# A linear-attention and two-MoE kernel on one core: the second part's preparation drawn one operation at a time, and new orders of the first loads and steps

## The chip, the cores and the metric

The kernel runs on one core of a Trainium2 chip. The time is the device time of one execution in microseconds, taken as the median of several runs. The engines named below are PE (TensorE), DVE (VectorE), ACT (ScalarE), POOL (GpSimd) and SP (SyncE, which issues all the DMAs here).

## What is computed

```python
kv  = einsum('bhsd,bhse->bhde', k, v);  o = einsum('bhsd,bhde->bhse', q, kv)     # 8 batches, 8 heads, 576 tokens, 64
x   = (o / sqrt(mean(o*o, -1) + 1e-6) * g_norm)  -> [4608, 512]
h   = x @ w_in                                             # [4608, 2048]
g   = (a0 + a1 h + a2 h^2 + a3 h^3) / (1 + |b0||h| + |b1|h^2 + 1e-6)
x2  = g @ w_out                                            # [4608, 512]
out = ((x2 @ w1) * (x2 @ w2) @ w3) @ w_out2                # [4608, 512]
```

The weights arrive in float64 and are turned into float32 on the chip. A float32 product is made of three passes, with each operand split into a rounded high part (`hi`) and a rest (`lo`): `hi*hi + hi*lo + lo*hi`.

## The kernel before

The program is written in a fixed order, and each engine works through its own list in that order. What an engine's next instruction needs from another engine is a semaphore wait, and everything behind it on the same engine waits too.

**The opening (lines 449 to 461)** is a string of letters, one operation each: `W` loads one weight block of 512 KB (float64, lines 99 to 115), `C` converts the next loaded block, `K` loads one tile of 128 tokens of k and v (512 KB), `Q` one of q (256 KB), `k` makes the tile's part of `kv` on PE, `t` transposes q, `o` multiplies it by `kv`, `r` and `n` normalise, `x` writes the split tile of x, `c` and `d` are constants, `F` finishes the pending conversions. A conversion is four steps (`to_f32`, lines 144 to 161): one on ACT (L149) and three on DVE (L151, L155, L159). The split of a converted block (L84 on ACT, L85 on DVE) follows when two more blocks have been converted. The k, v and q tiles have two buffers each, so the third `K` waits on SP until the first `k` has read its tile, and all loads behind it in SP's list wait with it. Eleven blocks are converted in the opening and 21 in the first 23 steps.

**The first MoE (lines 1103 to 1135)** goes through NG = 192 steps: 12 blocks of 384 tokens with 16 slices of the hidden width each. In step g PE makes `h` of slice g (`l1`, 12 matmuls) and adds slice g-3 to the four output accumulators (`l2`, 12 matmuls). `h` has two PSUM banks. Between them lies the rational function, written as generators that `mix` interleaves by a string of letters: `n` is `ew1` of slice g (three on ACT, L535 to L537; one on POOL, L539; then L542 and L544 on DVE, which read `h` from PSUM), `y` is `ewy` of slice g (two on ACT, after POOL), `s` is `ew2` of slice g-1 (L558, L560, L562 on DVE), `l` is `ew3` of slice g-2 (hi on ACT L525, lo on DVE L527), and `t`, `u`, `v` are conversions. `MIX` (line 1042) has one string for the first 23 steps and one for the rest; `CONV` (line 1043) says how many blocks are converted in each of the first 23 steps.

**The second part (lines 652 to 836)** multiplies x2 by w1 and w2 in `c_slot(n)`, 48 slots of seven products of six matmuls (five in the first slot). It is a fast 2x2 matrix scheme: seven combinations of the weights (A11, A12, A22, S1 to S4) and seven of the x2 blocks (B11, T1 to T4, B21, B22), each made by subtractions on DVE and a split (cast on ACT, rest on DVE). Slots 0 and 1 use the weights of `cw(0)`, 2 and 3 those of `cw(1)`. They take over the first MoE's buffers as these come free: the weights' combinations the `wa`/`wb` slots, the x2 pieces the x tiles and the buffers of the rational function.

**How this preparation is ordered before (lines 1065 to 1076).** LB = 176 is the first step of the last block. `prep` runs whole groups of operations at the head of a step, ahead of the step's own: loads at LB+1 and LB+7, the 11 operations of `cw(0)` in steps 185 to 190, the x2 pieces B11 in 187, the subtractions T3, T1, T2 in 188, the split T3 in 190, T1, T4's subtraction and T2 at 192. What is left is run inside `c_slot(0)` and `c_slot(1)` from `extra1` and `extra2`, between the products, all of `cw(1)` among it (in `c_slot(0)`). `c_slot(0)` stands in step 192, ahead of the last two `l2`; after the last one `x2_out` copies the four accumulators and stores them.

Of the kernel before, what the change touches and what calls it, by code (L numbers as in the profile page):

```python
# [8 lines left out]
F32 = mybir.dt.float32  # L9
# [3 lines left out]
AF = mybir.ActivationFunctionType  # L13
ALU = mybir.AluOpType
# [4 lines left out]
def linear_attention_two_moe_kernel(  # L19
# [24 lines left out]
    nc = tc.nc  # L44
# [4 lines left out]
    P = 128  # L49
# [4 lines left out]
    TA = 384  # L54
# [10 lines left out]
    wp = ctx.enter_context(tc.tile_pool(name="wp", bufs=1))  # L65
# [14 lines left out]
    def f32(ap):  # L80
        return ap.bitcast(F32)
# [325 lines left out]
    with tc.manual_schedule():  # L407
# [23 lines left out]
        def w_next():  # L431
            kind, i = w_seq[n_cv[0]]
            n_cv[0] += 1
            return (conv_a if kind == "a" else conv_b)(i)
# [16 lines left out]
            "r": (n_rms, n_rsq), "n": (n_out, x_pe), "x": (x_out,),  # L451
        }
        whole = {"W": w_load, "C": w_conv, "F": conv_flush, "c": consts, "d": const_ops}
        for op in "QKWQWKCWKWcCkCKKCQdtkWkktFktWCWooQoWWrCCWtWCoKWKrWnrkrKnCnQKkCxnxxWQCxWW":
            if op in whole:
                whole[op]()
            else:
                i = count.get(op, 0)
                count[op] = i + 1
                for f in tile_ops[op]:  # L460
                    f(i)
# [56 lines left out]
        def mt(tag, bufs, dt=F32):  # L518
            return mp.tile([P, TA], dt, tag=tag, name=tag, bufs=bufs)
# [55 lines left out]
        def do(g, place):  # L575
            for f, i in todo.get((g, place), ()):
                f(i)
# [69 lines left out]
        def sub(out, x, y):  # L647
            nc.vector.tensor_tensor(out=out, in0=x, in1=y, op=ALU.subtract)
# [4 lines left out]
        A11, A12, A22, S1, S2, S3, S4 = range(7)  # L653
        B11, T3, T1, T2, B21, T4, B22 = range(7)
        IP = 2
        cw = {}
        w12q = w12d.rearrange("(i s) p f -> s p i f", s=2)

        def cw_load(ip):
            def quad(t, row, half):  # L660
                nc.sync.dma_start(
                    out=t.rearrange("p (i f) -> p i f", i=IP),
                    in_=w12q[row][:, ip * IP:(ip + 1) * IP, half * 2 * P:(half + 1) * 2 * P],
                )
            e = cw[ip] = {m: slot(ip * 7 + m) for m in range(3)}
            for m, row, half in ((A11, 0, 0), (A12, 0, 1), (A22, 1, 1)):
                quad(f32(e[m][1]), row, half)
            t = wp.tile([P, 2, W], F32, tag=("wb0", "wb8", "wb9", "wb14")[ip], name="cwt")
            e["r"], e["t"] = t[:, 0, :], t[:, 1, :]
            quad(e["r"], 1, 0)  # L670

        def cw_work(ip):

            e = cw[ip]

            def to(m, t):
# [36 lines left out]

        raws = {}
# [3 lines left out]
        def raw_x(j, names=("11", "12", "22", "21")):  # L718
            if j >= NPR:
                return  # L720
            r = raws.setdefault(j, {})
            for name, tag, half, blk in RAW:
                if name not in names:
                    continue
                if tag:
                    r[name] = [atp.tile([P, TA], F32, tag=tag, name="xr", bufs=2) for _ in range(2)]
                else:
                    t = wp.tile([P, 2, TA], F32, tag="wb13" if j else "wb10", name="xr21")
                    r[name] = [t[:, kk, :] for kk in range(2)]
                for kk in range(2):  # L730
                    c0 = (2 * j + blk) * TA
                    nc.sync.dma_start(out=r[name][kk], in_=x2d[2 * half + kk, :, c0:c0 + TA])

        def gen_tmp(j):
            r = raws[j]
            t = wp.tile([P, 2, TA], F32, tag="wb14" if j else "wb7", name="xt3")
            r["tmp"] = [t[:, kk, :] for kk in range(2)]

        def gen_work(j):
# [299 lines left out]
                nc.scalar.copy(f["u"], f["b"])  # L1039
            e_load(n + 3)  # L1040

        MIX = "usnttulnslyutsntutu", "nltysstnnltts"
        CONV = "21102011020121111110011"
        NG = NBA * MF
        LB = NG - MF
        prep = {}
        extra1, extra2 = {}, {}

        def add(d, n, *fs):
            d.setdefault(n, []).extend(fs)  # L1050
# [3 lines left out]
        def take(key, *ns):  # L1054
            def f():
                if key not in work:
                    kind, n = key
                    work[key] = cw_work(n) if kind == "cw" else gen_work(n)
                for n in ns:
                    fs = work[key][n]  # L1060
                    for x in fs if isinstance(fs, list) else [fs]:
                        x()
            return f

        add(prep, LB + 1, lambda: raw_x(0, ("11", "12", "22")))
        add(prep, LB + 7, lambda: cw_load(0))
        for n in range(11):
            add(prep, LB + 9 + n // 2, take(("cw", 0), n))
        add(prep, LB + 11, take(("x", 0), 0))
        add(prep, LB + 12, take(("x", 0), 1, 2, 3))  # L1070
        add(prep, LB + 14, lambda: raw_x(0, ("21",)), take(("x", 0), 4))
        add(prep, NG - 1, lambda: cw_load(1))
        add(prep, NG, take(("x", 0), 5, 6, 7))
        add(extra1, 0, take(("x", 0), 8), take(("cw", 1), 0, 1, 2, 3, 4))
        add(extra2, 0, take(("cw", 1), 5, 6, 7, 8, 9, 10))
        add(extra1, 1, take(("x", 0), 9, 10), lambda: cw_load(2))
        add(extra2, 2, lambda: cw_load(3))
        for n, ip in ((2, 2), (4, 3)):
            add(extra1, n, take(("cw", ip), 0, 1, 2, 3))
# [2 lines left out]
        for j in range(NPR):  # L1082
# [8 lines left out]
            if j:  # L1091
                for c in range(5):
                    n = 5 * (j - 1) + c
# [7 lines left out]
        add(extra1, last + 7, lambda: w3_load(0))  # L1101

        for g in range(NG + SK):
            for f in prep.get(g, ()):
                f()
            do(g, 0)
            gens = {}
            if g < NG:
                l1(g)
                do(g, 1)  # L1110
                gens["n"] = ew1(g)
            if 0 <= g - 2 < NG:
                gens["l"] = ew3(g - 2)
            if g < NG:
                gens["y"] = ewy(g)
            if 0 <= g - 1 < NG:
                gens["s"] = ew2(g - 1)
# [8 lines left out]
            mix("".join(x for x in MIX[g >= len(CONV)] if x in gens), **gens)  # L1126
# [63 lines left out]
```

## Time and profile before

| | us |
|---|---|
| median of 3 runs | 1608.46 (1608.38 to 1609.85) |
| the profiled execution's own time | 1611.97 |
| its span, first to last instruction | 1609.6 |
| PE busy | 1532.3 (95%) |
| DVE busy | 1301.8 (81%) |
| ACT busy | 1057.8 (66%) |
| POOL busy | 230.1 (14%) |

Busy time is the time in which an engine had an instruction running. The granted clock is the share of full speed (2.4 GHz) that PE was given; its other level is one half (1.2 GHz). In the rows below a time at the head of a row is in microseconds from the start of the span, and the brackets at the end give the idle time of the engine ahead of that instruction and what released it.

### The profile page before, as it was taken

Reading aid. Unit: us, or ns where it says so; the run is one execution under the profiler, and the core shown is the slowest. Engines: PE = TensorE matmul, PEld = TensorE weight load, DVE = VectorE, ACT = ScalarE, POOL = GpSimd, SP = SyncE. Lnnn points to the kernel's source line nnn. Section 1 sums busy time; section 2 is a strip of 40 time slices with the busy share of each in tenths; the row PEclk is TensorE's granted clock in tenths of the full one; section 3 lists DMA queues with packets and bytes.
Section 4 is the critical chain, followed back from the end, with each engine's and each line's share of the span. In section 5 each row is a group of like instructions: output and inputs, shape, how many; then the busy total and the mean of one; then the engine's idle time right before and its main releaser. Section 6 shows DMA issues by size and latency. Waiting matters only on the chain.

```text
span 1609.6 us, 26146 instructions
## 1 busy us (share of the span) xinstructions
PE 1532.3 (95%) x9640; PEld 1482.0 (92%) x9640; DVE 1301.8 (81%) x2373; ACT 1057.8 (66%) x2109; POOL 230.1 (14%) x201
## 2 busy tenths in 40 slices
PE   3699999999999999999999997999999999999999
PEld 3588899999999999999999996999999998789999
DVE  3999977879899999999898989776676675578885
ACT  3588777778888888787888886444344343455554
POOL 0022121212222222222222221000000000000000
PEclk9699999999999999999999999999999999999999
DMA  9736234331111111111101011434533533344442
GB/s 258 206 99 168 63 95 112 86 92 45 42 44 52 47 37 47 46 53 27 53 27 55 6 47 36 151 109 150 184 125 125 183 116 130 118 131 158 158 158 86
DMA packets 202079, 157.93 MB, mean 98 GB/s; under 512 B 122848, under 2 KB 179936, under 8 KB 201952
## 3 DMA queue, kind: packets, MB, share of 16 engines
q1 hardware_dynamic: 201952, 156.28, 32.6%
q8 instruction: 75, 1.23, 0.3%
q14 instruction: 52, 0.43, 0.1%
HBM read 106.43 MB, written 49.81 MB: 97 GB/s over the span
## 4 chain that ended last, share of the span: by engine, by line
PE 71%; DVE 18%; ACT 5%; issue 3%; SPq 1%; POOL 1%; DMA 1%; DVEq 0%; ACTq 0%; POOLq 0%
PE acc L779 11%; PE h L88 6%; PE h L90 6%; PE h L89 6%; PE acc L492 5%; PE acc L987 5%; PE acc L489 5%; PE acc L490 5%; PE h L779 5%; PE kv L779 3%; PE at L779 3%; DVE n L560 3%; PE h L987 2%; DVE n L562 2%; DVE n L542 2%
## 5 line engine op out<-in xcount | busy, mean ns | idle before, releaser
L539 POOL TENSOR_TENSOR s<-z,a 128x384 f32<-128x384 f32 x192 | 228.5, 1190 | 759.5 <-ACT z L536 411.9
L560 DVE SCALAR_TENSOR_TENSOR n<-n,na,y 128x384 f32<-128x384 f32 x192 | 180.9, 942 | 0.0
L551 ACT ACTIVATE y<-s,epsq 128x384 f32<-128x384 f32 x192 | 118.4, 617 | 71.5 <-POOL s L539 70.9
L542 DVE TENSOR_TENSOR n<-n,h 128x384 f32<-128x384 f32 x192 | 104.8, 546 | 57.5 <-ACT n L537 57.0
L536 ACT ACTIVATE z<-a,ab 128x384 f32<-128x384 f32 x192 | 136.1, 709 | 6.4
L537 ACT ACTIVATE n<-h,na 128x384 f32<-128x384 f32 x192 | 126.0, 656 | 5.1 <-DVE lo L527 5.0
L535 ACT ACTIVATE a<-h 128x384 f32<-128x384 f32 x192 | 93.4, 487 | 54.3 <-PE h L90 52.9
L558 DVE SCALAR_TENSOR_TENSOR s<-s,y 128x384 f32<-128x384 f32 x192 | 125.1, 651 | 1.0
L544 DVE SCALAR_TENSOR_TENSOR n<-n,na,h 128x384 f32<-128x384 f32 x192 | 117.8, 613 | 6.0
L562 DVE SCALAR_TENSOR_TENSOR n<-s,n 128x384 f32<-128x384 f32 x192 | 105.8, 551 | 0.0
L527 DVE TENSOR_TENSOR lo<-n,hi 128x384 fp32r<-128x384 f32 x192 | 105.7, 551 | 0.0
L552 ACT ACTIVATE y<-y 128x384 f32<-128x384 f32 x192 | 101.0, 526 | 6.1
L525 ACT CAST hi<-n 128x384 fp32r<-128x384 f32 x192 | 96.3, 502 | 8.5 <-DVE n L562 8.3
L269 PEld LDWEIGHTS kv<-vt,kt 128*64 128x64 f32 (+1 forms) x640 | 25.1, 154 | 30.1 <-issue 21.3
L269 PE MATMUL kv<-vt,kt 128*64 128x64 f32 (+1 forms) x640 | 30.9, 246 | 20.0 <-DMA vt<-in_v_dram 18.1
L821 ACT COPY p<-kv 128x384 f32<-128x384 f32 x24 | 11.5, 479 | 41.3 <-PE kv L779 29.9
L821 ACT COPY p<-acc 128x384 f32<-128x384 f32 x24 | 11.5, 480 | 38.4 <-PE acc L779 33.0
L350 PE MATMUL at<-kvbd,qT 128*128 128x128 f32 (+1 forms) x216 | 28.9, 284 | 7.0 <-ACT qT L342 4.2
L350 PEld LDWEIGHTS at<-kvbd,qT 128*128 128x128 f32 (+1 forms) x216 | 26.6, 183 | 8.9 <-ACT qT L342 5.2
L836 ACT COPY u<-acc 128x384 f32<-128x384 f32 x24 | 11.5, 480 | 33.6 <-PE acc L779 33.6
L375 ACT ACTIVATE ny<-ms,epsn 128x8 f32<-128x8 f32 x36 | 11.1, 308 | 33.8 <-DVE ms L369 33.7
L796 DVE TENSOR_TENSOR acc<-acc,u 128x384 f32<-128x384 f32 x24 | 13.6, 566 | 19.2 <-ACT u L836 18.8
(1408 smaller groups left out, 4960.0 us busy)
## 6 DMA issues: line engine op xcount, KB each, us to landing
ed<-eo SPq DMA_DIRECT2D x48, 384.0 KB, 2.6
er<-ed SPq DMA_DIRECT2D x36, 512.0 KB, 3.8
x2d<-xev SPq DMA_DIRECT2D x48, 192.0 KB, 2.0
xr<-x2d SPq DMA_DIRECT2D x48, 192.0 KB, 4.2
out_dram<-o SPq DMA_DIRECT2D x36, 256.0 KB, 2.2
qt<-in_q_dram SPq DMA_DIRECT2D x32, 256.0 KB, 3.1
kt<-in_k_dram SPq DMA_DIRECT2D x32, 256.0 KB, 3.4
vt<-in_v_dram SPq DMA_DIRECT2D x32, 256.0 KB, 4.1
```

Source lines behind the costliest of these rows:

```text
L527: nc.vector.tensor_tensor(out=e["lo"], in0=e["n"], in1=f32(e["hi"]), op=ALU.subtract)
L536: nc.scalar.activation(out=z, in_=a, func=AF.Identity, scale=ab[:, 1:2], bias=ab[:, 0:1])
L537: nc.scalar.activation(out=n, in_=h, func=AF.Identity, scale=na[:, 3:4], bias=na[:, 2:3])
L539: nc.gpsimd.tensor_tensor(out=s, in0=z, in1=a, op=ALU.mult)
L542: nc.vector.tensor_tensor(out=n, in0=n, in1=h, op=ALU.mult)
L544: nc.vector.scalar_tensor_tensor(out=n, in0=n, scalar=na[:, 1:2], in1=h, op0=ALU.add, op1=ALU.mult)
L551: nc.scalar.activation(out=y, in_=e["s"], func=AF.Abs_reciprocal_sqrt, bias=epsq[:, 0:1])
L558: nc.vector.scalar_tensor_tensor(out=s, in0=s, scalar=EPS_Q, in1=y, op0=ALU.add, op1=ALU.mult)
L560: nc.vector.scalar_tensor_tensor(out=n, in0=n, scalar=na[:, 0:1], in1=y, op0=ALU.add, op1=ALU.mult)
L562: nc.vector.scalar_tensor_tensor(out=n, in0=s, scalar=2.0, in1=n, op0=ALU.subtract, op1=ALU.mult)
L779: nc.tensor.matmul(bank, lhsT=lh[:, sl], rhs=x, start=first and kk == 0 and n == 0, stop=kk == 1 and n == 2, skip_group_check=True,)
L987: nc.tensor.matmul(bank, lhsT=l[:, c, :], rhs=r, start=first and c == 0 and x == 0, stop=c == KH - 1 and x == 2, skip_group_check=True,)
```

## The change

There are three edits.

1. The opening has a new order of the same letters. The first weight block is now loaded ahead of the first k and v tile; three `K` stand ahead of the second weight block; the constants are loaded before the first conversion; the conversions of the second to the sixth block, the transposes and the normalisation are ordered anew. Ten of the eleven conversions stood ahead of the last `x` that the first `h` needs; now nine do.
2. The first 23 steps have a new string in `MIX` (in `n`, `u`, `n` first, where it was `u`, `s`, `n`) and a new `CONV` (again 21 conversions in all).
3. The preparation is one chain of 76 single operations in a fixed order (`UNITS`). Each unit has the first step in which it may start (its gate). From step 177 on, `t` in the step's string draws the next operation of the chain; `PREP` says how many are drawn at most in each step, and drawing stops at a closed gate. The last block has a third `MIX` string, in which L542 and L544 stand ahead of L527 and L560. What is left is run in `c_slot(0)`, `(1)` and `(2)`, up to a given unit. Two scratch tiles move to other slots (`wb1`, `wb2` for `wb7`, `wb10`).

```diff
-        for op in "QKWQWKCWKWcCkCKKCQdtkWkktFktWCWooQoWWrCCWtWCoKWKrWnrkrKnCnQKkCxnxxWQCxWW":
+        for op in "QWKKKWcCCdtQkQWKkKWWCFkCtkWkWCCCWoCtQWWrKtCooWronrrnknWxxKnxWKWCkKQQCxWW":
...
-        MIX = "usnttulnslyutsntutu", "nltysstnnltts"
-        CONV = "21102011020121111110011"
+        MIX = "nunutsstlyltstntuuu", "nltysstnnltts", "ntsnnltlsyttst"
+        CONV = "21011011120111120111110"
...
-        add(prep, LB + 1, lambda: raw_x(0, ("11", "12", "22")))
-        add(prep, LB + 7, lambda: cw_load(0))
-        for n in range(11):
-            add(prep, LB + 9 + n // 2, take(("cw", 0), n))
-        add(prep, LB + 11, take(("x", 0), 0))
-        add(prep, LB + 12, take(("x", 0), 1, 2, 3))
-        add(prep, LB + 14, lambda: raw_x(0, ("21",)), take(("x", 0), 4))
-        add(prep, NG - 1, lambda: cw_load(1))
-        add(prep, NG, take(("x", 0), 5, 6, 7))
-        add(extra1, 0, take(("x", 0), 8), take(("cw", 1), 0, 1, 2, 3, 4))
-        add(extra2, 0, take(("cw", 1), 5, 6, 7, 8, 9, 10))
-        add(extra1, 1, take(("x", 0), 9, 10), lambda: cw_load(2))
+        def c_first(ip):
+            yield from u_c(ip, "f1")
+            yield from u_c(ip, "f2")
+            yield from u_to(ip, S3, "r")
+            yield from u_to(ip, S1, "t")
+            yield from u_c(ip, "f3")
+            yield from u_in(ip, A11)
...
+        UNITS = [
+            (LB + 1, lambda: half(raw_x, 0, ("11", "12", "22"))),
+            (LB + 2, lambda: u_piece(B11, "11")),
+            (LB + 4, lambda: half(cw_load, 0)),
+            (LB + 4, lambda: u_sub("tmp", "22", "12")),
+            (LB + 5, lambda: u_sub("12", "12", "11")),
+            (LB + 5, lambda: u_sub("11", "22", "12")),
+            (LB + 7, lambda: c_first(0)),
+            (LB + 7, lambda: c_rest(0)),
+            (LB + 4, lambda: u_piece(T3, "tmp")),
+            (LB + 14, lambda: half(cw_load, 1)),
+            (LB + 5, lambda: half(raw_x, 0, ("21",))),
+            (LB + 7, lambda: u_sub("tmp", "11", "21")),
+            (NG, lambda: u_piece(T1, "12")),
+            (NG, lambda: u_piece(T2, "11")),
+            (NG + 1, lambda: u_piece(B21, "21")),
+            (NG, lambda: c_first(1)),
+            (NG + 2, lambda: u_piece(T4, "tmp")),
+            (NG + 2, lambda: u_piece(B22, "22")),
+            (NG, lambda: c_rest(1)),
+        ]
+        PREP = "0623342432431864785"
...
+        add(extra1, 0, u_upto(13))
+        add(extra2, 0, u_upto(15))
+        add(extra1, 1, u_upto(18), lambda: cw_load(2))
+        add(extra1, 2, u_upto(19))
...
+            if LB < g:
+                gens["t"] = u_some(int(PREP[g - LB]))
+            mix("".join(x for x in MIX[(g >= len(CONV)) + (g > LB)] if x in gens), **gens)
```

## Rows read from the trace of the kernel before

**Rows 1.** Busy time of each engine by stretch (us), then clock, DMA share, GB/s.
```profile
0.00:62.30 62.30, 29.13 (x227) 24.88 (x228) 34.93 (x68) 25.70 (x49) 2.17 (x10) 0.81 0.93 237
62.30:190.00 127.70, 114.97 (x766) 104.62 (x765) 125.70 (x226) 103.15 (x195) 31.95 (x23) 0.96 0.50 130
960.50:1009.50 49.00, 37.73 (x187) 35.10 (x186) 45.63 (x79) 31.87 (x63) 7.14 (x6) 0.93 0.09 30
```

**Rows 2.** Waits of DVE, 0 to 63 us: total, times, longest.
```profile
DVE wa0r L151 <- DMA wa0r<-in_moe_w_in_dram: 8.9, 1, 8.9
DVE wa2hl L85 <- ACT wa2hl L84: 4.1, 1, 4.1
DVE wa4r L155 <- ACT ct L149: 3.8, 1, 3.8
DVE wb0r L155 <- ACT ct L149: 3.0, 1, 3.0
DVE n L542 <- ACT n L537: 2.0, 1, 2.0
```

**Rows 3.** Timeline of PE and DVE, the first tile and weight blocks as they land.
```profile
6.31 1.12 PE L269 MATMUL kv<-vt,kt 128*64 128x64 f32 x16 [6.31 <-DMA vt<-in_v_dram]
...
8.87 0.43 DVE L151 TENSOR_SCALAR wa0r<-wa0r 128x512 int32<-128x512 uint32 x1 [8.87 <-DMA wa0r<-in_moe_w_in_dram]
...
18.92 0.43 DVE L151 TENSOR_SCALAR wa3r<-wa3r 128x512 int32<-128x512 uint32 x1 [1.26 <-DMA wa3r<-in_moe_w_in_dram]
```

**Rows 4.** Timeline of DVE: a conversion, a split, pairs of 384 columns.
```profile
41.05 0.42 DVE L151 TENSOR_SCALAR wa5r<-wa5r 128x512 int32<-128x512 uint32 x1
...
42.92 0.68 DVE L85 TENSOR_TENSOR wa4hl<-ct,wa4hl 128x512 fp32r<-128x512 f32 x1
...
992.61 1.02 DVE L85 TENSOR_TENSOR xq<-xr,xq 128x384 fp32r<-128x384 f32 x2
993.55 1.02 DVE L648 TENSOR_TENSOR xt<-xr,xr 128x384 f32<-128x384 f32 x2
```

**Rows 5.** Timeline of PE: starts of steps 181, 182 and 187, then of c_slots.
```profile
935.28 0.34 PE L88 MATMUL h<-xh,wa5hl 128*128 128x384 f32 x1
939.48 0.34 PE L88 MATMUL h<-xh,wa6hl 128*128 128x384 f32 x1
960.48 0.34 PE L88 MATMUL h<-xh,wa11hl 128*128 128x384 f32 x1
...
1009.50 0.34 PE L779 MATMUL acc<-xq,wa0hl 128*128 128x384 f32 x1
1018.96 0.34 PE L779 MATMUL at<-xq,wa7hl 128*128 128x384 f32 x1
1026.33 0.34 PE L779 MATMUL acc<-xq,wa7hl 128*128 128x384 f32 x1
```

**Rows 6.** Timeline of DVE and POOL: a free step, a loaded one, an early one.
```profile
938.91 1.02 POOL L539 TENSOR_TENSOR s<-z,a 128x384 f32<-128x384 f32 x1 [3.18 <-ACT z L536]
939.42 0.55 DVE L542 TENSOR_TENSOR n<-n,h 128x384 f32<-128x384 f32 x1 [1.06 <-ACT n L537]
...
955.88 1.38 DVE L560 SCALAR_TENSOR_TENSOR n<-n,na,y 128x384 f32<-128x384 f32 x1
...
129.32 3.26 POOL L539 TENSOR_TENSOR s<-z,a 128x384 f32<-128x384 f32 x1 [3.77 <-ACT z L536]
```

**Rows 7.** Timeline of PE and DVE, the last l2 and the first two c_slots.
```profile
1005.74 0.48 PE L489 MATMUL acc<-hi,wb15hl 128*128 128x384 f32 x1 [4.54 <-ACT hi L525]
...
1011.32 0.56 DVE L798 TENSOR_TENSOR c<-h,p 128x384 f32<-128x384 f32 x1 [4.56 <-DMA x2d<-xev]
...
1018.61 0.57 DVE L796 TENSOR_TENSOR acc<-acc,u 128x384 f32<-128x384 f32 x1 [1.01 <-ACT u L836]
...
1024.47 0.69 DVE L641 TENSOR_TENSOR wa14hl<-wa14hl 128x512 fp32r<-128x512 f32 x1 [1.06 <-ACT wa14hl L639]
...
1026.87 0.56 DVE L796 TENSOR_TENSOR h<-h,u 128x384 f32<-128x384 f32 x1
```

More of the change, by code (lines that the diff above doesn't have):

```diff
@@ L727, in raw_x @@
                 else:
-                    t = wp.tile([P, 2, TA], F32, tag="wb13" if j else "wb10", name="xr21")
+                    t = wp.tile([P, 2, TA], F32, tag="wb13" if j else "wb2", name="xr21")
                     r[name] = [t[:, kk, :] for kk in range(2)]
@@ L735, in gen_tmp @@
             r = raws[j]
-            t = wp.tile([P, 2, TA], F32, tag="wb14" if j else "wb7", name="xt3")
+            t = wp.tile([P, 2, TA], F32, tag="wb14" if j else "wb1", name="xt3")
             r["tmp"] = [t[:, kk, :] for kk in range(2)]
@@ L1040, in d_slot @@
             e_load(n + 3)
-        MIX = "usnttulnslyutsntutu", "nltysstnnltts"
-        CONV = "21102011020121111110011"
+        MIX = "nunutsstlyltstntuuu", "nltysstnnltts", "ntsnnltlsyttst"
+        CONV = "21011011120111120111110"
         NG = NBA * MF
         LB = NG - MF
-        prep = {}
         extra1, extra2 = {}, {}
@@ L1075, in linear_attention_two_moe_kernel, with half, cut @@
-        add(extra2, 0, take(("cw", 1), 5, 6, 7, 8, 9, 10))
-        add(extra1, 1, take(("x", 0), 9, 10), lambda: cw_load(2))
+        def half(f, *a):
+            f(*a)
+            yield
+        def cut(hi, lo, x, sign=1.0):
+            nc.scalar.activation(out=hi, in_=x, func=AF.Copy, scale=sign)
+            yield
+            if sign == 1.0:
+                nc.vector.tensor_tensor(out=lo, in0=x, in1=f32(hi), op=ALU.subtract)
+            else:
+                nc.vector.scalar_tensor_tensor(
+                    out=lo, in0=x, scalar=sign, in1=f32(hi), op0=ALU.mult, op1=ALU.subtract
+                )
+            yield
@@ new lines, in u_piece, with u_sub, u_c @@
+        def u_piece(m, name):
+            piece(0, m)
+            for kk in range(2):
+                yield from cut(*pieces[0, m][kk], raws[0][name][kk])
+        def u_sub(out, x, y):
+            r = raws[0]
+            if out == "tmp" and "tmp" not in r:
+                gen_tmp(0)
+            for kk in range(2):
+                sub(r[out][kk], r[x][kk], r[y][kk])
+                yield
+        def u_c(ip, k):
+            e = cw[ip]
+            if k == "f1":
+                nc.vector.tensor_tensor(out=e["t"], in0=e["r"], in1=f32(e[A22][1]), op=ALU.add)
+            elif k == "f2":
+                sub(e["r"], f32(e[A11][1]), e["r"])
+            elif k == "f3":
+                sub(e["t"], e["t"], f32(e[A11][1]))
+            elif k == "f4":
+                sub(e["t"], f32(e[A12][1]), e["t"])
+            yield
@@ new lines, in u_to, with u_in @@
+        def u_to(ip, m, name):
+            cw[ip][m] = slot(ip * 7 + m)
+            yield from cut(*cw[ip][m], cw[ip][name])
+        def u_in(ip, m, sign=1.0):
+            hi, lo = cw[ip][m]
+            yield from cut(hi, lo, f32(lo), sign)
+        def c_first(ip):
[5 more added lines that the diff above has]
+            yield from u_in(ip, A11)
@@ new lines, in c_rest @@
+        def c_rest(ip):
+            yield from u_to(ip, S2, "t")
+            yield from u_c(ip, "f4")
+            yield from u_in(ip, A12)
+            yield from u_to(ip, S4, "t")
+            yield from u_in(ip, A22, -1.0)
+        UNITS = [
[19 more added lines that the diff above has]
+        ]
@@ new lines, in linear_attention_two_moe_kernel, with u_chain, u_some @@
+        PREP = "0623342452431864785"
+        now = [0]
+        upos = [0]
+        def u_chain():
+            for k, (g, f) in enumerate(UNITS):
+                upos[0] = k
+                while now[0] < g:
+                    yield False
+                for x in f():
+                    yield True
+            upos[0] = len(UNITS)
+        chain = u_chain()
+        def u_some(n):
+            for i in range(n):
+                if not next(chain, False):
+                    break
+                yield
@@ L1077, in linear_attention_two_moe_kernel, with u_upto, f @@
+        def u_upto(k):
+            def f():
+                now[0] = NG + 9
+                while upos[0] < k and next(chain, False):
+                    pass
+            return f
+        add(extra1, 0, u_upto(13))
+        add(extra2, 0, u_upto(15))
+        add(extra1, 1, u_upto(18), lambda: cw_load(2))
+        add(extra1, 2, u_upto(19))
         add(extra2, 2, lambda: cw_load(3))
@@ L1103, in linear_attention_two_moe_kernel @@
         for g in range(NG + SK):
-            for f in prep.get(g, ()):
-                f()
+            now[0] = g
             do(g, 0)
@@ L1125, in linear_attention_two_moe_kernel @@
                 gens["t"] = bg_conv(BG_AT.index(g - 2))
-            mix("".join(x for x in MIX[g >= len(CONV)] if x in gens), **gens)
+            if LB < g:
+                gens["t"] = u_some(int(PREP[g - LB]))
+            mix("".join(x for x in MIX[(g >= len(CONV)) + (g > LB)] if x in gens), **gens)
             do(g, 2)
```

## The prediction

> **What bounds the kernel now.** I read the busy time of each engine by stretch first, because the whole span is an average over stages with different limits. It shows three stretches in which PE is not full. In the first 62.3 us DVE is busy for only 34.9 us [rows 1], and its waits say for whom it stood: loads at first, then three times ACT [rows 2]. From 62.3 to 190 us, which are the first 23 steps and the end of the conversions, DVE is busy for 125.7 of 127.7 us, so that stretch is DVE's. From 960.5 to 1009.5 us, the end of the last block, DVE is busy for 45.6 of 49.0 us and PE for 37.7, at a mean granted clock of 0.93 [rows 1]. Between these PE runs a step every 4.20 us (935.28 to 939.48) [rows 5], with DVE waiting 1.06 us of each for ACT [rows 6]. There nothing of the change applies. From slot 2 on a slot takes 7.37 us (1018.96 to 1026.33) [rows 5].
>
> **The opening.** A conversion holds DVE for 1.87 us (41.05 to 42.92) and a split for about 0.65 [rows 4]. The amount of work is the same in both orders, so what counts is DVE's idle time up to its first product with `h` at 62.3 us: now 62.3 - 34.9 = 27.4 us [rows 1]. Landings follow the bytes ahead of them in the one list on SP: 768 KB by 6.31 us, 1280 KB by 8.87, 4096 KB by 18.92 [rows 3], that is 3.66 us per 1024 KB. In the new order the first block has 768 KB up to its end and lands at 6.3. The second block stands behind the third `K`, which must wait for the buffer that the first `k` reads; that tile lands at 8.9 (1280 KB), its product takes 1.1 us [rows 3], so the third `K` is issued at about 10.0. It and the second block (1024 KB) land at about 15.5, with some 2 us for the empty queue to start (an estimate). Third block: 1024 KB later, 19.2. Fourth: 1536 KB later, 24.7. DVE's idle time is then 6.3 to start; 8.2 to 15.5 = 7.3; 17.4 to 19.2 = 1.8; then a conversion and three splits (3.8 us) to 23.0, and 1.7 to 24.7: together 17.1 us. From there the bytes are equal in both orders (5888 KB up to the fifth block), and DVE lags behind the loads. The three waits on ACT of now, 4.1 + 3.8 + 3.0 us, come from ACT standing behind PE's transposes and behind a normalisation whose sum DVE had not made [rows 2]. In the new order the flush `F` follows its conversion with no transpose between, and four conversions stand ahead of the first `r`. I leave one such wait (2.5 us) and 1.5 us of small ones; the 2.0 us wait for ACT at the first product [rows 2] goes, as two conversions and an `x` now stand ahead of it. New idle time 17.1 + 4.0 = 21.1 us, gain 6.3. Bounds: no wait at all gives 10.3; if the 4.1 and 3.8 us waits return, -1.6. PE's first `h` starts earlier too, but that buys nothing by itself, since DVE sets the next stretch.
>
> **The first 23 steps.** Conversions (21) and element-wise work are unchanged, and DVE has only 2.0 us of idle time to lose [rows 1]. What the order can alter is the collisions with POOL. A DVE operation that takes both operands from SBUF can last 1.38 us in place of 0.61 beside a POOL operation (0.77 more); L542, which takes one from PSUM, ran its 0.55 us beside one undisturbed; and in the early steps POOL also waited for DVE, 3.26 us in place of 1.02 [rows 6]. So the 23 POOL operations can cost DVE between 0 and 17.7 us in either order. The new order puts L542 in front, where a POOL operation can slip in, and an operation with two SBUF operands soon after it. I see no reason for a sign and take 0, with 6 us (a third of the bound) either way. The new `CONV` moves some conversions one step later; the last conversion still comes in step 21, and every split stands at least three steps ahead of the product that needs it, so I cost that at nothing; without this cover, a late block would hold PE for a conversion, 1.9 us.
>
> **The last block and the first slots.** From step 187 (960.48) to the start of slot 1 (1009.50) it takes 49.0 us [rows 5]. PE's own work there is five steps of 4.20, half a step, five products of 7.37 / 7 each, and two half steps: 21.0 + 2.1 + 5.3 + 4.2 = 32.6. Slot 1 takes 9.46 us in place of 7.37 [rows 5]. So 16.4 + 2.1 = 18.5 us are lost here now, 4.54 of them in one wait of PE for hi of the last slice [rows 7], which stands on ACT and DVE behind the whole of `cw(1)`. What is left of this loss with the change:
>
> - Steps 178 to 191. I follow the counts through the gates: drawn are 1, 2, 2, 3, 4, 0, 4, 3, 2, 4, 3, 1, 5, 4, 0, 7, 8, 5 in steps 177 to 194 (75 asked for, 58 drawn), then 6, 4 and 8 in the slots, 76 in all. So the chain does run out as written. In steps 178 to 191 that is 23 DVE operations: 12 on 384 columns at 0.47 us (992.61 to 993.55 for two) and 11 on 512 at 0.65 [rows 4], 12.8 us, against 14 x 1.06 = 14.8 us of DVE's free time [rows 6]. The free time lies beside POOL's operation, and if 5 of the 12 steps that draw DVE work pay 0.77 us [rows 6], 3.9 us come on top: 1.9 over, and unevenly spread. I take 2.5 us of PE's time, between 0 (no collision) and 7.2 (all 12 pay). The casts on ACT, one or two a step at about 0.6, have room beside it.
> - Step 192 and slot 0. T1's split can begin only when the last `l1` has read the x tile; `l2` and two products, 6.3 us, cover it. B21's cast stands on ACT behind the copy of the product before it, so the fifth product waits about 1 us, and what lag DVE brings adds as much: 2.0, between 0.8 and 4.
> - Slot 1. DVE's 4.56 us wait for the store of the accumulators [rows 7] stays, since that store still follows the last `l2` directly; T4 is ready earlier. Of the 2.1 us 0.7 stay.
> - Slots 2 and 3. Five DVE operations of `cw(1)`, 3.1 us, move into slot 2. DVE now needs from 1018.61 to 1026.87, 8.26 us with a wait of 1.06, for that slot's list [rows 7]: 7.2 + 3.1 = 10.3 in a slot of 7.37. Slot 3's third product waits behind it on DVE's additions to the accumulators. I take 1.5 us, between 0 and 3. Slot 3's own list is short enough to catch up.
>
> Left over are 2.5 + 2.0 + 0.7 + 1.5 = 6.7 of 18.5 us: gain 11.8, between 2.2 (18.5 - 7.2 - 4 - 2.1 - 3) and 17.0 (18.5 - 0 - 0.8 - 0.7 - 0). On SP the loads of weights and x pieces keep their place behind the store of block 10, and the second load of x waits for a slot until about step 187, four steps before the chain uses it; I cost the moved loads at nothing (a landing of 5 us would be that price).
>
> **Sum.** 6.3 + 0 + 11.8 = 18.1 us off the profiled execution's own 1611.97 us gives 1593.9. The median of the runs is 3.5 us lower, and so is the forecast: 1590.4 us, own range 1582 to 1599.
>
> **Rivals.**
>
> - The opening's gain doesn't arrive: one long wait on ACT returns, or collisions in the 23 steps eat it. For it: those steps are DVE's with no room [rows 1]. Against: 27.4 us of idle time is much to lose again. Only the second part's gain is left: 1608.5 - 11.8 = 1596.7.
> - The drawn operations all collide with POOL, so that the last block stays DVE's. For it: the free time lies just where POOL works [rows 6]. Against: in the loaded early steps it was POOL that waited [rows 6]. Losses at their ends, 7.2 + 4 + 0.7 + 3 = 14.9, leave 3.6; with the opening 9.9 off: 1598.6. The Trainium skill, page "SBUF — State Buffer", section "Who interferes with whom", states this case as a rule: a DVE instruction with two SBUF inputs and a GpSimd instruction that reads SBUF exclude each other, and whichever issues second stands for the whole of the first. The 1.38 us row bears it out, and the rule would give this rival's time if POOL always came first.
> - More than forecast: no ACT waits in the opening and fewer collisions in the 23 steps (6 us). 10.3 + 6 + 11.8 = 28.1: 1580.4.
> - Slower than before: with L542 in front of DVE's list, each of the 23 steps begins with a wait for ACT's three operations, as the free steps show it, 1.06 us [rows 6]. 23 x 1.06 = 24.4, and 1608.5 - 18.1 + 24.4 = 1614.8. It decides from 18.1 / 23 = 0.79 us a step. Against: DVE is busy for 98% of that stretch [rows 1] and ACT for 81%, so ACT runs ahead.
>
> **How the numbers follow.** Forecast 0.52, rivals in their order 0.20, 0.12, 0.10 and 0.06. The range leaves out the slower rival and part of the fastest: 1580 to 1603. 0.2% is 3.2 us, about what can be told from no change here. All cases but the last are faster by more than that, but I move 0.04 from them to no change, as the first two rivals could come together. Faster 0.90, same 0.04, slower 0.06.
>
> **What would show it.** DVE busy by 40 us should rise well above now's, the first `h` start near 50 us, and step 23 about 6 us earlier than now. From step 187 to slot 1 I expect about 37 us (49.0 now), no wait of PE for hi of the last slice above 1 us, and a wait of 1 to 2 us in slot 3. The prediction is wrong if the steps up to 191 run at more than 4.6 us on average, if step 23 does not start earlier, or if DVE waits for ACT at L542 in the first 23 steps.

## The result and the profile after

The changed kernel takes 1589.0 us (median of 4 runs, 1586.1 to 1590.0), the kernel before 1608.4: a ratio of 0.987, with an interval of 0.9845 to 0.9891, which is 19.4 us off. The profiled executions took 1589.95 and 1611.97 us. One of the four executions of e4 below ran at a mean granted clock of 0.75 and took 1868.3 us; e4's median is that of the other three.

The first view is again the busy time of each engine by stretch, of the kernel after: up to DVE's first product with `h` (L542), from there to step 23, from step 187 to slot 1, and slot 1.

```profile
0.00:58.68 58.68, 28.34 (x227) 23.90 (x228) 34.35 (x67) 24.79 (x48) 2.17 (x10) 0.91 0.95 228
58.68:179.05 120.37, 108.50 (x743) 99.89 (x742) 115.83 (x224) 100.80 (x192) 30.02 (x23) 0.97 0.57 149
950.29:985.18 34.89, 33.99 (x187) 31.96 (x186) 33.82 (x63) 28.83 (x59) 7.75 (x6) 1.00 0.06 19
985.18:993.11 7.93, 7.74 (x43) 7.42 (x43) 4.74 (x10) 3.89 (x9) 0.00 (x0) 1.00 0.79 257
```

Against [rows 1], DVE is idle for 24.3 us ahead of its first L542, where it was 27.4; and the end of the last block takes 34.9 us in place of 49.0, with PE busy for 34.0 of them and the granted clock at 1.00 in place of 0.93. The second stretch has to be set against the same one of before, which ends at step 23 and not at 190 us:

```profile
62.31:186.09 123.78, 111.06 (x744) 100.70 (x743) 121.79 (x220) 100.07 (x189) 31.57 (x23) 0.96 0.51 134
```

DVE did four instructions more in the changed kernel and was busy for 6.0 us less. Starts of PE's steps and slots in the kernel after, which answer to [rows 5] and to the 4.54 us wait of [rows 7]:

```profile
179.05 0.34 PE L88 MATMUL h<-xh,wa15hl 128*128 128x384 f32 x1
950.29 0.34 PE L88 MATMUL h<-xh,wa11hl 128*128 128x384 f32 x1
972.68 0.44 PE L489 MATMUL acc<-hi,wb13hl 128*128 128x384 f32 x1 [0.72 <-ACT hi L525]
985.18 1.32 PE L779 MATMUL acc<-xq,wa0hl 128*128 128x384 f32 x6
993.11 1.22 PE L779 MATMUL at<-xq,wa7hl 128*128 128x384 f32 x6
1000.48 1.22 PE L779 MATMUL acc<-xq,wa7hl 128*128 128x384 f32 x6
1004.50 0.94 PE L779 MATMUL h<-n,wa9hl 128*128 128x384 f32 x4 [1.75 <-DVE c L798]
1009.83 1.22 PE L779 MATMUL at<-xq,wa14hl 128*128 128x384 f32 x6
```

The rows are steps 23 and 187, the only wait of PE between step 187 and slot 1 (0.72 us), then the starts of slots 1, 2, 3 and 4, with a wait of 1.75 us in slot 3, the main place where the change costs something. Followed along the span, after minus before in the profiled executions:

| point | before | after | difference |
|---|---|---|---|
| DVE's first L542 | 62.31 | 58.68 | -3.6 |
| step 23 | 186.09 | 179.05 | -7.0 |
| step 27 | 210.23 | 199.88 | -10.4 |
| step 187 | 960.48 | 950.29 | -10.2 |
| slot 1 | 1009.50 | 985.18 | -24.3 |
| slot 4 | 1033.70 | 1009.83 | -23.9 |
| end of the span | 1609.6 | 1587.1 | -22.5 |

Some 10 us come ahead of step 27 and some 14 from the end of the last block. Between steps 27 and 187 the two differ by 0.2 us. From slot 4 to the end no run here has an edit, and yet this part takes between 573.7 us (e1) and 578.6 (e8) in the thirteen traces, 575.9 in before and 577.3 after; so the 1.4 us that are lost again there are within what traces differ by.

### The profile page after: what moved, and what is told of

Same layout as the page of the kernel before. It is cut to its first block, busy times and chain, and to the rows that moved or that the text cites. A ratio compares the mean times of both kernels' runs of the same rounds, so it can differ in the third digit from the quotient of the medians.

```text
span 1587.1 us, 26153 instructions
## 1 busy us (share of the span) xinstructions
PE 1524.4 (96%) x9640; PEld 1475.7 (93%) x9640; DVE 1290.3 (81%) x2373; ACT 1055.4 (66%) x2109; POOL 230.2 (15%) x201
## 4 chain that ended last, share of the span: by engine, by line
PE 71%; DVE 17%; ACT 6%; issue 3%; POOL 1%; DMA 1%; SPq 1%; DVEq 0%; ACTq 0%; POOLq 0%
PE acc L779 11%; PE h L88 7%; PE h L90 6%; PE h L89 6%; PE acc L492 5%; PE acc L987 5%; PE acc L489 5%; PE acc L490 5%; PE h L779 5%; PE at L779 3%; PE kv L779 3%; DVE n L560 2%; PE h L987 2%; PE kv L987 2%; DVE lo L527 2%
## 5 line engine op out<-in xcount | busy, mean ns | idle before, releaser
L539 POOL TENSOR_TENSOR s<-z,a 128x384 f32<-128x384 f32 x192 | 228.6, 1190 | 742.5 <-ACT z L536 419.3
L560 DVE SCALAR_TENSOR_TENSOR n<-n,na,y 128x384 f32<-128x384 f32 x192 | 179.2, 933 | 0.0
L542 DVE TENSOR_TENSOR n<-n,h 128x384 f32<-128x384 f32 x192 | 104.9, 547 | 51.8 <-ACT n L537 51.2
L558 DVE SCALAR_TENSOR_TENSOR s<-s,y 128x384 f32<-128x384 f32 x192 | 125.3, 653 | 0.9
L544 DVE SCALAR_TENSOR_TENSOR n<-n,na,h 128x384 f32<-128x384 f32 x192 | 118.0, 614 | 6.0
L527 DVE TENSOR_TENSOR lo<-n,hi 128x384 fp32r<-128x384 f32 x192 | 106.0, 552 | 0.0
L269 PEld LDWEIGHTS kv<-vt,kt 128*64 128x64 f32 (+1 forms) x640 | 25.1, 153 | 25.5 <-issue 20.4
L269 PE MATMUL kv<-vt,kt 128*64 128x64 f32 (+1 forms) x640 | 30.9, 246 | 15.5 <-DMA vt<-in_v_dram 12.1
L375 ACT ACTIVATE ny<-ms,epsn 128x8 f32<-128x8 f32 x36 | 11.1, 308 | 32.6 <-DVE ms L369 32.5
L796 DVE TENSOR_TENSOR acc<-acc,u 128x384 f32<-128x384 f32 x24 | 13.6, 566 | 19.2 <-ACT u L836 18.8
```

The lines of the kernel that those rows point to most:

```text
L527: nc.vector.tensor_tensor(out=e["lo"], in0=e["n"], in1=f32(e["hi"]), op=ALU.subtract)
L539: nc.gpsimd.tensor_tensor(out=s, in0=z, in1=a, op=ALU.mult)
L544: nc.vector.scalar_tensor_tensor(out=n, in0=n, scalar=na[:, 1:2], in1=h, op0=ALU.add, op1=ALU.mult)
L558: nc.vector.scalar_tensor_tensor(out=s, in0=s, scalar=EPS_Q, in1=y, op0=ALU.add, op1=ALU.mult)
L560: nc.vector.scalar_tensor_tensor(out=n, in0=n, scalar=na[:, 0:1], in1=y, op0=ALU.add, op1=ALU.mult)
```

## The experiments

"Excess" below is the time by which long DVE operations of a stretch (more than 0.05 us over the lower quartile of their line and shape) lasted longer than that quartile; an operation of 1.38 us where 0.61 is usual [rows 6] adds 0.77. I call them collisions with POOL: each of them overlaps an L539 in its trace. Such operations cost time only where DVE sets the pace: in steps 27 to 176 the excess is 78 us in before and in the changed kernel alike, 104 long operations, and PE still runs a step every 4.20 us. Free time of DVE is the length of the stretch less its busy time.

**Each edit alone** (e1 to e3, on the kernel before).

```diff
e1:  opening string of the change; MIX, CONV and preparation as before
e2:  first string of MIX and CONV of the change; the rest as before
e3:  chain (UNITS, PREP) and third string of MIX; the rest as before
```

> The kernel before with the new order of the opening alone. Theory (the three edits add up, each in its own stretch): DVE's first product with h starts 3.6 us earlier than in the kernel before (58.7 in place of 62.3, as in the changed kernel), step 23 starts 3 to 4 us earlier, and the time is 3 to 5 us below before, 1604 to 1606. Rival (the opening's gain is used up in the first 23 steps, and the 7 us by which step 23 is earlier in the changed kernel are all of the new step strings): step 23 starts within 1 us of before, time 1607 to 1609.

> The kernel before with the new string and the new counts of conversions for the first 23 steps alone. Theory (collisions of DVE with POOL): the time that DVE's operations last over their usual length in the first 23 steps falls from 11 us to about 2 to 3, step 27 starts 5 to 8 us earlier than in the kernel before (210.2), time 1600 to 1604. Rival (what counts is where the opening ends): collisions stay near 11 us without the new opening, step 27 within 2 us of before, time 1606 to 1609.

> The kernel before with the chain alone (and its third string). Theory: from step 187 to the start of slot 1 it takes 35 us in place of 49.0, slot 1 takes 7.9 in place of 9.5, slot 3 9.3 in place of 7.4, together 13 to 14 us, time 1594 to 1597. Rival (the second part gains only if it starts in the state that the earlier edits leave): less than 10 us.

| kernel | median us | ratio to before | first L542 | step 23 | step 27 | 187 to slot 1 | excess, first 23 steps |
|---|---|---|---|---|---|---|---|
| before | 1609.1 | | 62.3 | 186.1 | 210.2 | 49.0 | 11.1 (21 long) |
| e1 | 1607.4 | 0.9978 to 0.9997 | 59.0 | 182.7 | 204.8 | 49.1 | 10.2 (21) |
| e2 | 1604.0 | 0.9963 to 0.9983 | 60.5 | 181.1 | 202.0 | 49.3 | 2.3 (6) |
| e3 | 1595.4 | 0.9902 to 0.9931 | 62.4 | 186.0 | 208.1 | 34.9 | 10.3 (21) |

The opening alone brings its 3.4 us to step 23, but only 1.7 us of the time (0.5 to 3.5 by the interval), less than I had expected; what becomes of the rest is not shown. The steps' edit alone brings 5.1 us, with most of the collisions gone. The mark "first L542" moves with the string too: e2 has it 1.8 us earlier with the opening of before. The chain brings 13.6, as expected. The three add to 20.4 us, the whole to 19.4: they are nearly independent. The trace of e3 also tells of one accident: its code in steps 23 to 26 is that of before, and it passes them in 22.08 us where before took 24.14. The first two rows are the same stretch, 192 to 199 us, of before and then of e3; the other three are a wait of PE in step 23, of before, e3 and the changed kernel:

```profile
192.00:199.00 7.00, 5.92 (x27) 5.92 (x28) 6.00 (x12) 4.67 (x9) 1.27 (x2) 0.76 0.35 75
```

```profile
192.00:199.00 7.00, 6.50 (x40) 6.47 (x41) 6.93 (x12) 5.72 (x11) 2.24 (x2) 1.00 0.35 76
```

```profile
193.08 0.33 PE L393 MATMUL at<-ident,xt 128*128 128x128 f32 x1 [2.02 <-DVE xt L386]
```

```profile
192.50 0.33 PE L393 MATMUL at<-ident,xt 128*128 128x128 f32 x1 [1.50 <-DVE xt L386]
```

```profile
184.25 0.33 PE L393 MATMUL at<-ident,xt 128*128 128x128 f32 x1 [0.23 <-DVE xt L386]
```

In before PE ran part of it at the lower clock (0.76 on average) and did 27 matmuls in place of 40. Of the 2.06 us between before and e3, 0.52 are the longer wait; the other 1.5 are the price of the lower clock (an estimate from these rows; e5, with a wait of 2.12 us there and no lower clock, takes 22.69 for the stretch). So some 1.5 us of the 10.4 up to step 27 belong to that one execution of before, which was also 3.5 us above its median. The wait itself goes with the steps' edit: it is 1.50 us in e1 as in e3, and 0.26 in e2, near the changed kernel's 0.23.

**The two halves of the steps' edit** (e5 and e6, on the kernel before).

```diff
e5:
-        MIX = "usnttulnslyutsntutu", "nltysstnnltts"
+        MIX = "nunutsstlyltstntuuu", "nltysstnnltts"
e6:
-        CONV = "21102011020121111110011"
+        CONV = "21011011120111120111110"
```

> The kernel before with the new string for the first 23 steps, and the old counts of conversions. Theory (the string alone takes the collisions away): operations of DVE last 2 to 4 us over their usual length in the first 23 steps in place of 11, step 27 starts 5 to 7 us earlier than in the kernel before, time 1603 to 1605. Rival (the counts do it, by leaving fewer steps with two conversions and none in the last step): collisions 8 us or more, time 1607 to 1609.

> The kernel before with the new counts of conversions, and the old string. Theory (the string does it): collisions stay at 9 to 12 us, time 1606 to 1609. Rival (the counts): collisions 4 us or less, step 27 starts 4 us or more earlier, time 1603 to 1605.

e5 takes 1611.1 us against 1609.0 (ratio 1.0003 to 1.0022), e6 1611.6 (0.9999 to 1.0022). With the new string alone the excess falls to 2.9, as the theory said, and yet nothing is gained: both theories missed the time. The stretch from the first L542 to step 23, of e5:

```profile
61.81:186.32 124.51, 111.22 (x743) 102.83 (x743) 115.19 (x221) 99.86 (x191) 27.89 (x23) 0.95 0.50 134
```

DVE is busy for 6.6 us less than before and is free for 9.3 us in place of 2.0. Its waits in these steps (total, times, longest), of e5 and then of the changed kernel:

```profile
DVE n L542 <- ACT n L537: 10.0, 9, 2.6
```

```profile
DVE n L542 <- ACT n L537: 3.4, 3, 2.1
```

So L542 in front does wait for ACT: 2.6 us in step 0, and 6.1 of the rest in steps 4, 6, 9, 20 and 21, each right behind a step with no conversion. The old `CONV` has six steps without a conversion, often two in a row or close together; the new one spreads five, and only three waits are left, in steps 0, 3 and 6. With the counts alone (e6) the excess stays, 11.8, as its theory said, though the time lies 2.6 us above its range. Only both together gain: the string takes most of the collisions away, and with the new counts the waits for ACT fall from nine to three. That they do so because DVE's list is then long enough for ACT to be ahead is read from where the waits stand; no run tests it by itself.

**The old string in the last block** (e4, on the changed kernel).

```diff
-        MIX = "nunutsstlyltstntuuu", "nltysstnnltts", "ntsnnltlsyttst"
+        MIX = "nunutsstlyltstntuuu", "nltysstnnltts", "nltysstnnltts"
```

> The changed kernel with the old string of the later steps in the last block too; the chain is drawn by it, four operations inside the string and the rest at its end. Theory A (spreading the single operations over the steps is what counts): step 187 to slot 1 takes 35 to 37 us, time 1588 to 1592. Theory B (the new string counts, since L558 and L560 no longer stand together ahead of L542 in the time of POOL's operation): collisions in the last block rise from 2.4 us to 6 or more, step 187 to slot 1 takes 39 to 43 us, time 1593 to 1599.

1597.5 us (0.9911 to 0.9944), 8.4 above the changed kernel. Steps 178 to 186, of the changed kernel and then of e4:

```profile
912.18:950.29 38.11, 38.11 (x217) 37.59 (x217) 35.28 (x68) 32.72 (x64) 10.93 (x9) 1.00 0.22 70
```

```profile
911.84:955.00 43.16, 39.69 (x217) 37.25 (x217) 39.56 (x68) 34.23 (x65) 10.64 (x10) 1.00 0.19 62
```

The same 217 matmuls and 68 DVE operations take DVE 4.3 us more, and PE stands for 3.5 us, where it did not stand in the changed kernel. A further 2.7 us go from step 187 to slot 1 (37.6 for 34.9). The time is what the second theory forecast; the stretch it named was not (37.6 us where it had 39 to 43). From step 178 to slot 1 before takes 87.0 us, e4 80.7 and the changed kernel 73.0: the chain drawn by the old string is worth some 6 us there, the new string some 8 more. One step of the changed kernel shows how, DVE first and then POOL:

```profile
928.58 0.55 DVE L648 TENSOR_TENSOR xr<-xr 128x384 f32<-128x384 f32 x1
929.05 0.56 DVE L558 SCALAR_TENSOR_TENSOR s<-s,y 128x384 f32<-128x384 f32 x1
929.52 0.55 DVE L542 TENSOR_TENSOR n<-n,h 128x384 f32<-128x384 f32 x1
930.11 0.61 DVE L544 SCALAR_TENSOR_TENSOR n<-n,na,h 128x384 f32<-128x384 f32 x1
...
928.81 1.68 POOL L539 TENSOR_TENSOR s<-z,a 128x384 f32<-128x384 f32 x1 [2.79 <-DVE n L562]
```

and the same place of e4, with the step after it:

```profile
929.66 1.37 DVE L558 SCALAR_TENSOR_TENSOR s<-s,y 128x384 f32<-128x384 f32 x1
...
935.40 1.38 DVE L560 SCALAR_TENSOR_TENSOR n<-n,na,y 128x384 f32<-128x384 f32 x1
...
929.41 1.20 POOL L539 TENSOR_TENSOR s<-z,a 128x384 f32<-128x384 f32 x1 [3.55 <-DVE n L562]
935.16 1.20 POOL L539 TENSOR_TENSOR s<-z,a 128x384 f32<-128x384 f32 x1 [4.54 <-DVE n L562]
```

In the changed kernel POOL's operation lasts 1.68 us and DVE loses nothing. Its usual 1.02 us [rows 6], counted back from its end at 930.49, begin at 929.47, where L542 does (929.52); so it seems to stand while L648 and L558 run, and to run beside L542 and L544, which read `h` from PSUM (an estimate from these rows). In e4 operations with two SBUF operands meet it, and DVE pays. From step 178 to slot 1 that comes to 12 long operations in e4 and 2 in the changed kernel. What the rows do not show is who goes first: L558 begins 0.24 us behind POOL in the changed kernel and 0.25 in e4, and lasts 0.56 us there and 1.37 here. The Trainium skill, page "SBUF — State Buffer", section "Who interferes with whom", says that a DVE instruction with at most one SBUF input, outside the 2-port perf modes, does not contend with GpSimd; 0.55 and 0.61 us for L542 and L544 beside POOL agree with that. One SBUF input alone is no cover here: L151, with one, lasted 1.24 us in before (at 98.75, beside POOL) where 0.43 is usual; whether it ran in such a mode no run shows.

**Where the rest of the opening and slot 3 stand** (e7, e8, on the changed kernel), and the changed kernel once more beside combinations (e9 to e11).

```diff
e7:
-  "QWKKKWcCCdt...
+  "QWKKWKcCCdt...
e8:
-        add(extra1, 2, u_upto(19))
+        add(extra2, 1, u_upto(19))
e9:   no edit
e10:  e7 and e8
e11:  e8 and
-  "QWKKKWcCCdtQkQWKkKWWCFk...
+  "QWKWKWKcCCdtQkQWKkKWCFk...
```

> The changed kernel with the second weight block loaded ahead of the third tile of k and v. Theory (the second block comes late because the third tile waits for its buffer, and DVE's idle time in the opening is paid one for one): DVE's 7.3 us wait for that block falls to 2 to 4 us, its first product with h starts 1 to 3 us earlier than 58.7, time 1 to 3 us below the changed kernel's 1589. Rival (the bytes are the same, so the later blocks come later by what the second gains): the waits for the third and fourth block grow by as much, first product within 0.7 us of 58.7, time unchanged.

> The changed kernel with the last eight operations of the chain run near the end of slot 1 in place of slot 2. Theory (slot 3 waits because slot 2's list on DVE is too long by what the chain adds): slot 3 takes 7.4 to 7.7 us in place of 9.35, slot 1 stays within 0.7 us of 7.92, time 1 to 2 us below the changed kernel's 1589. Rival (the wait only moves, as slot 1 then has the long list): slots 1 to 3 together stay within 0.5 us of 24.64.

> The changed kernel once more, as the measure for the next two. Theory (its stretches repeat): step 187 to slot 1 34.9 us, slot 3 9.35 us, time 1587 to 1590. Rival (its first result was a lucky set of half-clock stretches in the opening): 1592 or more.

> The changed kernel with the last eight operations of the chain near the end of slot 1, and the second weight block loaded ahead of the third tile. Theory (only the first of the two pays): time 1.5 to 2.5 us below the changed kernel of this set, first product with h within 0.7 us of it. Rival (both pay): 3 us or more below.

> As the kernel with the eight operations in slot 1, and the second and third weight block loaded ahead of the second and third tile of k and v. Theory (the opening is bound by the bytes up to the fifth block, 5888 KB in every order, so loads can only trade one of DVE's waits for another): DVE's waits for loads together stay within 2 us of 19, first product with h between 57.5 and 59.5 us, time within 2 us of the kernel with the eight operations in slot 1 alone (1587.4). Rival (DVE can be fed sooner): waits for loads 15 us or less, first product at 56 us or earlier, time 1584 or less.

| kernel | median us | ratio to before | first L542 | step 23 | slots 1 to 3 |
|---|---|---|---|---|---|
| after, with the kernel of the result | 1589.0 | 0.9845 to 0.9891 | 58.7 | 179.1 | 24.6 |
| e9 | 1588.9 | 0.9861 to 0.9894 | 58.5 | 178.8 | 24.7 |
| e7 | 1587.5 | 0.9848 to 0.9877 | 59.2 | 179.9 | 24.7 |
| e8 | 1587.4 | 0.9843 to 0.9876 | 59.2 | 179.7 | 22.8 |
| e10 | 1587.7 | 0.9855 to 0.9884 | 59.1 | 179.3 | 22.8 |
| e11 | 1584.5 | 0.9836 to 0.9866 | 58.2 | 178.8 | 22.8 |

DVE's longest waits up to its first L542, of the changed kernel, then of e7, then of e11:

```profile
DVE wa1r L151 <- DMA wa1r<-in_moe_w_in_dram: 7.3, 1, 7.3
DVE wa0r L151 <- DMA wa0r<-in_moe_w_in_dram: 5.6, 1, 5.6
DVE wa3r L151 <- DMA wa3r<-in_moe_w_in_dram: 3.1, 1, 3.1
DVE wa2r L151 <- DMA wa2r<-in_moe_w_in_dram: 3.0, 1, 3.0
DVE wb2r L155 <- ACT ct L149: 1.3, 1, 1.3
```

```profile
DVE wa0r L151 <- DMA wa0r<-in_moe_w_in_dram: 5.9, 1, 5.9
DVE wa2r L151 <- DMA wa2r<-in_moe_w_in_dram: 4.6, 1, 4.6
DVE wa1r L151 <- DMA wa1r<-in_moe_w_in_dram: 4.1, 1, 4.1
DVE wa3r L151 <- DMA wa3r<-in_moe_w_in_dram: 2.5, 1, 2.5
```

```profile
DVE wa0r L151 <- DMA wa0r<-in_moe_w_in_dram: 6.5, 1, 6.5
DVE kvbd L288 <- ACT kvbd L287: 4.4, 1, 4.4
DVE na L215 <- DMA co_a<-in_moe_a_dram: 4.3, 1, 4.3
DVE wa1r L151 <- DMA wa1r<-in_moe_w_in_dram: 1.3, 1, 1.3
```

With the second block one letter earlier (e7) its wait falls by 3.2 us and the third block's rises by 1.6, with small ones behind it; the first L542 comes no earlier. With the weights first (e11) the wait for the second block falls to 1.3 and two others of 4.4 and 4.3 come. The rival of e7 holds: DVE's idle time in the opening changes its place, not its sum (24.3 us up to the first L542 in the changed kernel, 24.7 in e7, 23.8 in e11). e11's theory fails in two of its three points: DVE's waits for loads come to 13.9 us, below even the 15 of its rival, where 17 to 21 were forecast, and the time is 2.9 us below e8's in place of 2 at most. The first L542 comes at 58.2, as the theory had it, since the 4.4 us wait for ACT stands in their place.

The changed kernel repeats (e9): 34.9 us from step 187 to slot 1, 9.36 in slot 3. In e8 the wait in slot 3 is gone. All that PE still waits for between 985 and 1010 us is

```profile
PE h L779 <- DVE c L798: 0.2, 1, 0.2
```

and slot 3 takes 7.37 us (9.35), for 0.14 more in slot 2. By the trace that is 1.8 us gained; the times of e7, e8 and e10 lie 1.2 to 1.6 us below the changed kernel's, inside the intervals, so none of the three gains is shown by the time; e10's 1.2 is also below the 1.5 to 2.5 forecast for it. e11 is the fastest version measured: 1584.5, in one set with e9's 1588.9. It beats the kernel before; its interval and e9's touch (0.9861 to 0.9866). Of the 4.4 us between them its trace accounts for 1.8 in the slots; e8's and e11's stretches agree within 1 us up to slot 4, and their medians, which come from different sets, differ by 3. What the rest of it is stays open, also because e11's profiled execution was its slowest of four (1588.3): its trace does not hold the gain that the median shows.

## Why the prediction was right

The forecast of 1590.4 us is 1.4 above the median, and the median lies inside both ranges. Its terms were less good than the sum: one was too large, one that I had set to nothing was not nothing, and these nearly cancel. To that extent the closeness of the total is luck.

- **The opening: right in kind, 6.3 us forecast, 3.6 measured** at DVE's first L542 (3.3 in e1, the opening by itself), within its bounds. The landings went wrong at their end. DVE took up the first block at 5.6 us (6.3 forecast), the second at 15.1 (15.5), the third at 20.4 (19.2) and the fourth at 27.4 (24.7). The rows of SP's list in the changed kernel:

```profile
5.39 1.01 SPq L242 DMA_DIRECT2D vt<-in_v_dram  x1
9.28 0.37 SPq L242 DMA_DIRECT2D kt<-in_k_dram  x1
...
10.32 0.77 SPq L104 DMA_DIRECT2D wa1r<-in_moe_w_in_dram  x1
...
14.75 1.44 SPq L104 DMA_DIRECT2D wa2r<-in_moe_w_in_dram  x1
...
17.95 2.77 SPq L242 DMA_DIRECT2D kt<-in_k_dram  x2
...
22.12 0.62 SPq L104 DMA_DIRECT2D wa3r<-in_moe_w_in_dram  x1
```

The columns are the start of an issue and its length; the issues left out stand between the rows shown. The third `K` waited until 9.3 us, as argued (10.0). What I had not reckoned with is what follows: from 9.3 to 22.1 us SP issues with gaps of 0.1 us at most, 0.4 to 2.1 us each (a row with x2 is two issues), and the fourth block is issued only at 22.1. The 2 us that I had put down as an estimate, for the empty queue to start, came out: from the third `K`'s issue to the second block it is 5.8 us, 2.1 more than 3.66 for its 1024 KB. From the second block's landing to the fourth's there are 2560 KB in 12.3 us, 4.9 us per 1024 KB where I took 3.66. Whether the issues slow the transfers or full queues the issues, no run here tells apart. DVE's waits for the four blocks are 19.0 us in all (17.1 forecast), and 5.3 us of idle time are left beside them (4.0). The long waits on ACT went, as forecast: one of 1.3 us and 0.7 at the first product are left of 4.1, 3.8, 3.0 and 2.0 [rows 2]. DVE was busy for 19.1 of the first 40 us (15.7 before). The first `h` started at 53.5 us, not near 50.

- **The first 23 steps: "no reason for a sign" was the step that failed.** I took 0 within 6 us either way. The excess fell from 11.1 to 2.3 us (e2 alone: 2.3), and DVE's free time rose by 2.5, so that step 23 came 7.0 us earlier, 3.4 more than the opening's 3.6 (near the 6 of the forecast only because these two errors cancel). A further 3.3 us come in steps 23 to 26: 1.5 the stretch at the lower clock in before's execution, and 1.8 the wait of PE for DVE that fell from 2.02 to 0.23 us, which I had not priced either. I had both halves of the mechanism ([rows 6]: L542 undisturbed beside POOL, 1.38 us for an operation with two SBUF operands), and had written that the new order lets POOL slip in at L542; I then said that an operation with two SBUF operands follows soon after, without counting in which order the two come. The string decides that, and it is readable from the code. By line, most of before's excess lies in conversions: 8 long L159 of 1.25 to 1.35 us where 0.68 is usual, 4.7 us in all; L560 and L558 have 3.2, L151 and L85 1.6 each. In the changed kernel one long L159 is left, of 1.40. Groups of these lines in this stretch (operations, busy us, mean ns), of before and then of after:

```profile
L560 DVE SCALAR_TENSOR_TENSOR n<-n,na,y 128x384 f32<-128x384 f32 x22 | 14.7, 668 | 0.0
L558 DVE SCALAR_TENSOR_TENSOR s<-s,y 128x384 f32<-128x384 f32 x22 | 13.9, 633 | 0.0
L159 DVE SCALAR_TENSOR_TENSOR ct<-ct,wb5r 128x512 int32<-128x512 int32 x1 | 1.4, 1352 | 0.0
```

```profile
L560 DVE SCALAR_TENSOR_TENSOR n<-n,na,y 128x384 f32<-128x384 f32 x21 | 12.9, 613 | 0.0
L558 DVE SCALAR_TENSOR_TENSOR s<-s,y 128x384 f32<-128x384 f32 x22 | 12.4, 564 | 0.0
L159 DVE SCALAR_TENSOR_TENSOR ct<-ct,wb4r 128x512 int32<-128x512 int32 x1 | 1.4, 1403 | 0.0
```

The new `CONV` at nothing was also a wrong reading: alone it is worth nothing (e6), but without it the string gains nothing either (e5).

- **The last block and the slots: right, 11.8 us forecast, 13.7 measured** in the trace and 13.6 in e3. I had 2.5 us left over in steps 178 to 191, with 5 of 12 steps colliding, and 2.0 in step 192 and slot 0. Steps 178 to 186 took 38.1 us, 0.3 over nine times 4.20, and step 187 to slot 1 took 34.9 against 32.6 of PE's own work: 2.6 in place of 4.5. The collisions that I priced do come, but with the old string: e4 has an excess of 9.5 us from step 178 to slot 1 against 1.7. Part of before's loss was also the clock, which the sum did not separate: two stretches of 3.4 us at half speed, at most 1.7 us each (an estimate), which the changed kernel does not have. Slot 1 has 0.55 us left (0.7 forecast) and slot 3 2.0 (1.5): DVE's list for slot 2, forecast at 10.3 us, ran from 992.77 to 1003.20, 10.4. PE's wait for hi of the last slice is gone (the 0.72 us one is for slice 13); the 37 us that I expected from step 187 to slot 1 were 34.9. One reading was wrong without harm to the sum: DVE's 4.56 us wait for the store of the accumulators did not stay, it is 0.63. The store still lands 1.9 us after its issue (1009.33 to 1011.20 before, 985.16 to 987.01 after), but DVE now comes to it 1.4 us after the issue and came 2.6 us ahead of it.

```profile
992.77 0.57 DVE L796 TENSOR_TENSOR acc<-acc,u 128x384 f32<-128x384 f32 x1 [1.01 <-ACT u L836]
...
1003.20 0.56 DVE L796 TENSOR_TENSOR h<-h,u 128x384 f32<-128x384 f32 x1
```

- **The rivals.** That the opening's gain doesn't arrive is out as far as step 23, where e1 has 3.4 us; of the time it shows 1.7. That all drawn operations collide is out for this string; with the old one (e4) the time is 1597.5, near the 1598.6 worked out for it, and the collisions are there. The slower rival was not an idle one: L542 does wait for ACT with the new string, 10.0 us in e5, 0.4 us a step where 0.79 would have decided. I named DVE's wait at L542 as a sign of a wrong prediction; three such waits came, and cost less than the collisions that went.
- **Profiled executions and medians.** From the profiled execution I took 18.1 us; by the profiled executions 22.0 went, by the medians 19.4. I moved the forecast by the 3.5 us between before's profiled execution and its median, which proved right: the low clock in steps 23 to 26 was 1.5 us of it.

## What to carry to other kernels

Where DVE and POOL share work, read from the order string which DVE operation stands where POOL's starts, and put those with an operand in PSUM there, where DVE sets the pace: that was worth some 8 us of the time in the last block. An order that puts a waiting operation first needs enough work behind the engine that feeds it, so such an order and the amount of work per step are tried together, not one at a time. When loads stand in one list, check the rate taken from one stretch of it on a second stretch with another mix of loads.

## What the runs showed of the hardware that was not expected

PE's clock fell behind waits of PE, but not behind each one. Before has a stretch at the lower clock from 193.6 us, right behind the 2.02 us wait that ended at 193.08, and e6 has one at the same place behind 2.28 us; in e5 a wait of 2.12 us there has none behind it, nor have the 1.50 us of e1 and e3. The two that before has at 978.7 and 1006.0, 3.4 us each, come right behind waits of 3.41 us for lo (to 978.01) and 4.54 for hi (to 1005.74). All five traces with the old preparation (before, e1, e2, e5, e6) have both, and none of the eight with the chain has one from step 187 to slot 1, where the changed kernel's PE waits for 0.7 us in all and the clock is 1.00 throughout. So a wait that is taken away can give back more than its length.

A comparison of two single traces is good to some 2 us over a stretch like steps 23 to 26, and to 5 us over the part from slot 4 to the end.
